# Pooled attention and maxout FFN: a hand-ordered program with groups of 64 tokens, the attention output of batches 2 to 7 transposed by the DMA crossbar

## The chip, the cores and the metric

One core of a Trainium2 chip. The time is the device time of one execution in microseconds (us); each kernel ran several times, in rounds beside the kernel before on the same chip. The kernel before took 288.1 to 290.7 us in all its executions. An execution over 1.5% above the fastest of its kernel is called slow; ratios use the others, the fast ones, alone. "The profile" is one execution taken by the hardware profiler; "the trace" is its list of instructions and transfers. Engines: PE = TensorE (PEld its weight loads), DVE = VectorE, ACT = ScalarE, POOL = GpSimd, SP = SyncE, which has no busy time on either page and issues transfers (161 before, 104 after the change). "SPq" or "ACTq" in a line is the transfer queue of that engine.

## The reference

K and V are averaged over 8 neighbouring tokens (576 become 72), each of 8 heads attends to the 72, and the result goes through three matrices whose products are maximised, and an output matrix.

```
q, k, v: (8 batches, 8 heads, 576, 64)          tokens: 8*576 = 4608, width 512
k_p, v_p = mean of 8 neighbours                 (8, 8, 72, 64)
attn = softmax(q @ k_p.T / 8)                   (8, 8, 576, 72)
x = (attn @ v_p), heads side by side            (4608, 512)
h = max(x @ w1, x @ w2, x @ w3)                 (4608, 768)
out = h @ w_out                                 (4608, 512)
```

## The kernel before

It works batch by batch: load, fold K and V over 8 neighbours (`fold`), transpose queries and keys, scores and exponentials (`heads`), products with V, normalisation and a TensorE transpose into `xT` (`values`). When 512 tokens are in `xT`, a group `moe(n)` follows: 72 matmuls with w1, w2, w3, then 24 with w_out. A scheduler orders each engine's instructions. These parts matter for the argument; cuts are marked.

```python
def load(b, after=None):
    kt = ld.tile([96, 6, POOL, D], F32, name="kt", tag="kt")      # ld: two buffers
    ...
    loads = [nc.sync.dma_start(out=kt, in_=ksrc)]                  # SyncE's queue
    loads.append(nc.sync.dma_start(out=vt, in_=vsrc))
    nc.gpsimd.dma_start(out=qb, in_=...)                           # converts to bf16
...
fold(nc.gpsimd, kt, [kp2[:, :, 0, :], kp2[:, :, 1, :]])            # b >= 2, on POOL
fold(nc.gpsimd, vt, [vp_all[:, b, :, 0:D]])
...
def values(b, ets):                                                # per chunk of 128 tokens
    ...                                                            # 8 matmuls, reciprocal
    xn = sb3.tile([128, 2, 4, D], F16, name="xn", tag="xn")        # sb3: three buffers
    nc.vector.tensor_tensor(out=xn, in0=..., in1=..., op=ALU.mult)
    for kc in range(KCH):
        nc.tensor.transpose(pxt[:, kc, :], xn[...], identh)        # four transposes
    nc.scalar.copy(out=xT[:, :, g0 + keep:g0 + 128], in_=pxt[:, :, keep:128])
...
def moe(n):
    ...                        # w1 part copied by ScalarE, two maxima by VectorE, then w_out
    for u in range(4):
        nc.sync.dma_start(out=dst[:, g, :], in_=osb[32 * u:32 * u + 32, :])
...
for b in range(B):
    loaded = first if b == 0 else load(b, w_dma[2])                # behind the weights
```

The softmax here doesn't subtract the row's maximum and nothing guards it: scores larger than these inputs give would overflow.

## Time and profile before

| | before |
|---|---|
| time, median | 289.3 us |
| profiled span | 288.2 us |
| first product with w1 starts | 43.97 us |
| last matmul ends | 281.3 us |
| TensorE's work between, at undisturbed distances | 226.4 of 237 us |
| SyncE's queue waiting for POOL's folds | 33 us |

The profile falls into a start that TensorE spends waiting for weights and keys, a body in which it is full, and an end of stores. The prediction shows the lines and reads them. "Undisturbed distance" is the time from the start of one matmul to the start of the next in a full stream (0.216 us at 512 columns, 0.056 us at 128). It is the measure used for TensorE throughout, as the durations that the profile gives overlap in a full stream: 379 ns for one of 512 columns, 219 ns for a transpose of 128 (medians).

### The profile page before, as it was taken

What the parts mean: (1) busy time and instruction counts of PE and PEld (TensorE: products, weight loads), DVE (VectorE), ACT (ScalarE), POOL (GpSimd) and SP (SyncE); (2) the same over time, 40 slices, a digit from 0 to 9 for tenths busy, and PEclk for the clock granted to TensorE, in tenths of its full rate; (3) what the DMA queues carried; (4) which work ended last, traced back from release to release, by engine and by line L of the source; (5) the groups of instructions that cost most, each with busy time, mean ns of one, the idle gap of its engine ahead of it and who ended that gap; (6) DMA issues with size and microseconds to landing.
All of it is one profiled execution on the core that took longest, in us unless ns stands there. A gap on an engine that the chain in (4) does not pass through costs nothing.

```text
span 288.2 us, 4331 instructions
## 1 busy us (share of the span) xinstructions
PE 248.6 (86%) x1664; PEld 131.2 (46%) x1664; DVE 129.3 (45%) x224; ACT 128.0 (44%) x218; POOL 117.4 (41%) x68
## 2 busy tenths in 40 slices
PE   0254049999999999999999999999999999999990
PEld 0132044564545455545554565456455544444440
DVE  7420083483238334724571557057505832533520
ACT  1134024753575267535753663565357533222230
POOL 6048006999999999999282300000000000000000
PEclk9999999999999999999999999999999999999996
DMA  7999999898839959975912700320040005014013
GB/s 189 255 228 199 261 239 229 190 219 234 193 111 216 202 141 214 235 174 119 206 31 72 141 20 0 98 50 0 2 123 23 2 9 138 1 27 120 3 45 102
DMA packets 17190, 36.47 MB, mean 127 GB/s; under 512 B 2736, under 2 KB 5040, under 8 KB 16496
## 3 DMA queue, kind: packets, MB, share of 16 engines
q1 hardware_dynamic: 12624, 28.32, 38.6%
q0 software_dynamic: 4544, 7.87, 15.3%
q8 instruction: 13, 0.21, 0.3%
q14 instruction: 9, 0.07, 0.1%
HBM read 34.60 MB, written 9.44 MB: 153 GB/s over the span
## 4 chain that ended last, share of the span: by engine, by line
PE 77%; DMA 14%; ACT 2%; DVE 1%; issue 1%; POOL 1%; SPq 0%; ACTq 0%; POOLq 0%
PE pw L194 47%; PE po L211 15%; DMA mw<-in_moe_w_dram 7%; PE psc L152 6%; PE pxt L179 4%; DMA out_dram<-osb 4%; DMA kt<-in_k_dram 3%; PE pav L166 3%; PE pqt L128 3%; ACT xT L183 2%; PE pkt L137 1%; DVE kt L108 1%; POOL mw L88 1%; ACT osb L215 0%; DVE xn L174 0%
## 5 line engine op out<-in xcount | busy, mean ns | idle before, releaser
L194 PE MATMUL pw<-xT,mw 128*128 128x512 f16 x648 | 163.8, 382 | 0.7 <-ACT xT L183 0.7
L194 PEld LDWEIGHTS <-mw 128*128 128x128 f16 x648 | 60.4, 98 | 51.0 <-issue 1.1
L202 DVE TENSOR_TENSOR t<-t,pw 128x512 f16<-128x512 f16 x54 | 37.1, 687 | 100.0 <-PE pw L194 97.6
L108 POOL TENSOR_TENSOR vt<-vt 72x2048 f32<-72x2048 f32 (+1 forms) x16 | 54.8, 3427 | 36.3 <-DMA vt<-in_v_dram 35.7
L199 ACT CAST t<-pw 128x512 f16<-128x512 f32 x54 | 31.6, 585 | 48.2 <-PE pw L194 47.7
L211 PE MATMUL po<-mwo,hT 128*128 128x512 f16 x216 | 48.1, 379 | 0.0
L205 DVE TENSOR_TENSOR hT<-t,pw 128x512 f16<-128x512 f16 x54 | 37.1, 686 | 16.5 <-PE pw L194 13.8
L155 ACT ACTIVATE et<-psc 72x576 f16<-72x576 f32 x64 | 37.4, 645 | 11.4 <-PE psc L152 11.3
L215 ACT COPY osb<-po 128x512 f32<-128x512 f32 x36 | 21.1, 587 | 36.2 <-PE po L211 34.7
L183 ACT COPY xT<-pxt 128x512 f16<-128x512 f16 (+1 forms) x40 | 21.8, 544 | 33.5 <-PE pxt L179 33.3
L211 PEld LDWEIGHTS <-hT 128*128 128x128 f16 x216 | 21.1, 98 | 25.5 <-DVE hT L205 1.7
L108 POOL TENSOR_TENSOR kt<-kt 96x1536 f32<-96x1536 f32 (+1 forms) x12 | 31.4, 2617 | 0.4
L152 PE MATMUL psc<-qT,kz 128*72 128x288 bf16 x128 | 27.9, 304 | 2.4 <-ACT et L155 1.5
L133 ACT COPY qT<-pqt 128x768 bf16<-128x768 bf16 x23 | 18.4, 801 | 24.0 <-PE pqt L128 23.7
L174 DVE TENSOR_TENSOR xn<-pav,rcp 128x512 f16<-128x512 f32 x40 | 26.7, 684 | 0.4
L179 PE MATMUL pxt<-identh,xn 128*128 128x128 f16 x160 | 16.5, 229 | 11.4 <-DVE xn L174 10.8
L128 PE MATMUL pqt<-ident,qb 128*128 128x128 bf16 x144 | 13.2, 234 | 13.7 <-DMA qb<-in_q_dram 12.0
L152 PEld LDWEIGHTS <-kz 128*72 128x72 bf16 x128 | 14.0, 117 | 19.5 <-issue 8.8
L179 PEld LDWEIGHTS <-xn 128*128 128x128 f16 x160 | 11.9, 102 | 21.9 <-DVE xn L174 17.4
L166 PE MATMUL pav<-vp,et 72*128 72x65 f16 x320 | 18.8, 200 | 3.3 <-POOL vp L111 3.3
L128 PEld LDWEIGHTS <-qb 128*128 128x128 bf16 x144 | 10.9, 105 | 20.5 <-DMA qb<-in_q_dram 12.0
L166 PEld LDWEIGHTS <-et 72*128 72x128 f16 x320 | 15.6, 103 | 7.3 <-ACT et L155 3.2
(23 smaller groups left out, 72.9 us busy)
## 6 DMA issues: line engine op xcount, KB each, us to landing
vt<-in_v_dram SPq DMA_DIRECT2D x8, 1152.0 KB
out_dram<-osb SPq DMA_DIRECT2D x144, 64.0 KB, 1.7
kt<-in_k_dram SPq DMA_DIRECT2D x7, 1152.0 KB, 10.4
qb<-in_q_dram POOLq DMA_DIRECT2D x8, 576.0 KB, 12.1
mw<-in_moe_w_dram POOLq DMA_DIRECT2D x3, 768.0 KB, 18.3
kt<-in_k_dram SPq DMA_DIRECT2D x2, 576.0 KB, 6.8
mwo<-in_moe_w_out_dram POOLq DMA_DIRECT2D x1, 768.0 KB, 25.4
```

Of the source, the lines that this page charges most:

```text
L108: e.tensor_tensor(out=t[:, :, 0:n, :], in0=t[:, :, 0:n, :], in1=t[:, :, n:2 * n, :], op=ALU.add)
L128: nc.tensor.transpose(pqt[:, u, :], qb[:, g, 2 * i:2 * i + 2, :], ident)
L152: nc.tensor.matmul(psc[:, par, 0:288], kz[:, par, h, :], mov, start=True, stop=True)
L155: nc.scalar.activation(out=et.rearrange("p (i a r) -> p i a r", a=2, r=NR), in_=psc[:, :, 0:288].rearrange("p a (i r) -> p i a r", r=NR), ...
L166: nc.tensor.matmul(pav[:, h // 4, 65 * (h % 4):65 * (h % 4) + 65], ets[h][:, c0:c0 + 128], vp_all[:, b, h, :], start=True, stop=True)
L179: nc.tensor.transpose(pxt[:, kc, :], xn[:, kc // 2, 2 * (kc % 2):2 * (kc % 2) + 2, :], identh)
L183: nc.scalar.copy(out=xT[:, :, g0 + keep:g0 + 128], in_=pxt[:, :, keep:128])
L194: nc.tensor.matmul(pw, w_sb[wi][:, kc, bass.ts(jc, 128)], xT[:, kc, col], start=(kc == 0), stop=(kc == KCH - 1))
L199: nc.scalar.copy(out=t, in_=pw)
L202: nc.vector.tensor_tensor(out=t1, in0=t, in1=pw, op=ALU.max)
L205: nc.vector.tensor_tensor(out=hT[:, jc, :], in0=t, in1=pw, op=ALU.max)
L211: nc.tensor.matmul(po, hT[:, jc, bass.ts(mm, 128)], wo_sb[:, jc, :], start=(jc == 0), stop=(jc == JCH - 1))
```

## The change

Its intent: start the first group earlier, by loading in smaller pieces in the order of need and by fixing every engine's order by hand; take stores in pieces of 64 rows; and take the transposes of the output off TensorE from batch 2 on. The crossbar transposes go out from SyncE, so the loads of K and V of batches 2 to 7 moved to ScalarE's queue. The diff, cut to what the argument touches:

```diff
-    NR = 32                                  # tokens of a query group
+    NR = 64
+    ctx.enter_context(tc.manual_schedule())  # program order is kept on each engine
...
+    for i in range(3):
+        load_w(slice(256 * i, 256 * i + 256))          # weights in thirds
...
-            kz[128, 2, H, 72]                          # keys as weights
+            kz[128, 2, H, 128]
...
+    def turn_x(b, c0, keep, xn, tag):
+        if b > 1:
+            g0 = S * b + c0
+            nc.sync.dma_start_transpose(
+                out=xT[:, :, g0 + keep:g0 + 128],
+                in_=xn.rearrange("p g h d -> p (g h d)")[keep:128])
+            return
+        ...                                            # batches 0 and 1: TensorE, as before
...
+    loads_on = nc.scalar
+    def load(b):
+        kts[b], x = load_kv(b, "kt", k, loads_on, F32, 1)
+        vts[b], y = load_kv(b, "vt", v, loads_on, F32, 1)
+        ...
+        load_q(b)
+    for slot, _ in enumerate(project(0, hT0)):         # output part of group 0
+        ...
+    load(2)
+    load(3)
+    fold_k(2, nc.gpsimd)
+    fold_v(2)
+    ...
+    for n in range(1, TOK // NB):                      # groups 1 to 8
+        if n + 2 < B:
+            fold_k(n + 2, nc.gpsimd)
+            fold_v(n + 2)
+        if n + 3 < B:
+            load(n + 3)
+        ...
+        for part in (hidden(n, hT), project(n, hT)):   # one "slot" per step of the group
+            for _ in part:
+                next(side, None)
+                ...                                    # a step of batch n + 1
+                slot += 1
```

## The prediction

> **What bounds the kernel now.** I read the page's busy line and its slices first, because they say which engine to count and when it starts.
>
> ```profile
> PE 248.6 (86%) x1664; PEld 131.2 (46%) x1664; DVE 129.3 (45%) x224; ACT 128.0 (44%) x218; POOL 117.4 (41%) x68
> ...
> PE   0254049999999999999999999999999999999990
> ```
>
> TensorE is full from the seventh slice to the last but one; before that, in some 44 us, it does little. Two phases, then: a start that is bound by something else, and a body bound by TensorE. The chain of waits, in order of time, names the something else and shows the pace of the body:
>
> ```profile
> 4.47 21.32 DMA mw<-in_moe_w_dram
> 25.81 9.92 DMA kt<-in_k_dram
> ...
> 43.97 0.59 PE pw L194
> ...
> 276.09 5.19 PE po L211 x24
> ```
>
> The start waits for weights and then for keys held back behind them; the first product with w1 starts at 43.97 us. The last line gives the true cost of a 512-column matmul in a full stream: 5.19/24 = 0.216 us, not the 0.38 us that the group list shows as one's duration (that one includes the pipeline). Distances between starts in the same trace give 0.056 us for a 128-column transpose, 0.122 us for a 288-column score, 0.033 us for a value product of 65 columns. From 43.97 us to the last matmul's end at 281.3 us these distances account for 226.4 of 237 us; the other 11 us are small gaps, the largest sort (36 times about 0.08 us) ahead of scores with 72-column weights. The end, from the timeline:
>
> ```profile
> 278.03 7.56 SPq L219 DMA_DIRECT2D out_dram<-osb  x16
> 281.35 0.59 ACT L215 COPY osb<-po 128x512 f32<-128x512 f32 x1 [0.75 <-PE po L211]
> ```
>
> Sixteen stores of 64 KB go out one after the other at 0.47 us, so the span ends 6.9 us after the last matmul. The reported time is 1.1 us over the profiled span (289.3 against 288.2).
>
> Two more views matter for what the change moves: POOL's folds of V by shape, and what the DMA queue on SyncE waited for.
>
> ```profile
> L108 POOL TENSOR_TENSOR vt<-vt 72x2048 f32<-72x2048 f32 x8 | 36.1, 4508 | 35.7 <-DMA vt<-in_v_dram 35.7
> L108 POOL TENSOR_TENSOR vt<-vt 72x1024 f32<-72x1024 f32 x8 | 18.8, 2347 | 0.6
> L111 POOL TENSOR_TENSOR vp<-vt 72x512 f16<-72x512 f32 x8 | 10.1, 1267 | 0.6
> ...
> SPq L66 <- POOL kp L111: 16.7, 2, 9.1
> SPq L67 <- POOL vp L111: 16.6, 3, 8.3
> ```
>
> A fold of V costs 8.1 us of POOL. The loads of K and V into a double buffer wait for such folds (33 us in five waits). This costs nothing today: only stores stand behind them, on a queue that computes nothing.
>
> [...] 72-column weights load in 117 ns, 128-column ones in 98 ns.
>
> **The change part by part.**
>
> 1. *Start.* K, Q and V of batch 0 are loaded first, then the weights in column thirds, and the first two groups' first products run on half groups. Loading cost from the packets: converting packets take 98, 134 and 191 ns for 1024, 1536 and 2304 bytes written, a line of 23 + 0.073 ns per byte, so about 61 ns for the new 512-byte packets and 107 for 1152. Over 16 engines, q, k and v of batch 0 cost 3.4 + 3.2 + 3.5 us, one third of the weights 5.8 us. With packets of the converting queue starting near 6 us, batch 0 is in by some 13 us and the first third by some 20. Behind that: exponentials of batch 0 until about 18, then two output chunks (reciprocal 0.2, multiply 0.68, transpose, copy 0.59). **First product at about 22.5 us**, 21.5 earlier.
> 2. *Group 0.* 72 products x 0.216 = 15.6, three remaining chunks of batch 0 1.5, pooling K of batch 1 on TensorE (8 x 0.216) 1.7, its query transposes 1.0, waits 1.7: to 44. By the same packet sum w_out lands near 42 to 44. Output part: 24 x 0.216 = 5.2, scores 2.0, pooling V (16 half-width) 1.7, waits 1.5: to 54.4; its last copy ends at about **55**.
> 3. *The new wait.* In the built order of the changed kernel the loads of batches 2 and 3 stand on **ScalarE's** queue behind that copy (SyncE is kept for the transposes), and the loads of batch 4 at the head of group 1, waiting for POOL, ahead of the first evacuation of group 1. Batch 4 reuses the buffers of batch 2, so ScalarE stands still until batch 2 is loaded (6.5 us: 0.4 issue, 4.6 for 576 packets of 2 KB at about 128 ns on 16 engines, the rest latency), K folded (now 72 x 2048: 4.5 + 2.35 + 2 x 1.27 = 9.4) and V folded (8.1): 24 us. Then a copy, a maximum and two key copies (0.4 + 0.4 + 1.5) before TensorE goes on: **27 us**, of which TensorE uses 3.3. Later loads wait for folds that ended long before.
> 4. *TensorE's remaining work* after 55 us: 8 groups x 96 x 0.216 = 165.9; six batches at 18 x 0.056 + 8 x 0.033 + 8 x 0.25 + 40 x 0.033 = 4.6, in all 27.5; batch 1's outputs 2.4: 195.8, less the 3.3. The crossbar removes 120 transposes x 0.056 = **6.7 us** from TensorE and 30 copies of 0.37 to 0.59 us from ScalarE, which wasn't the bound.
> 5. *Gaps.* The 78 ns ones go with 128-column keys. But in a fixed order the first query transposes come one slot (0.86 us) after the key transposes whose two copies take 1.5 us; with the following query copies about 1.5 us per batch. I take 10 us in all, as now.
> 6. *End.* Two stores instead of four behind the last copy: 5 us instead of 6.9.
>
> Sum: 55 + 27 + 192.5 + 10 + 5 = 289.5; 1 for late transposes; 1.1 for the reported time: **291.5 us**. So the start gains 21.5, the end 2, the transposes 6.7, and almost all of it goes into one wait.
>
> **The rivals.** (a) *The wait is short or absent*, because loads land or folds run sooner than I think. POOL's fold times are steady in the trace (4.49 and 4.51 us), and the built order is plain, which speaks against it; without the wait, the sum would be about 267. Half of it would give 279. (b) *The crossbar is slow.* A chunk's normalised output has three buffers, so the fourth waits on VectorE for the first's transpose; between them are five slots, about 4.2 us of slack. With a latency of 7 us VectorE, and soon TensorE, would lose some 2 us in each of six batches: about 303. Nothing in the trace before speaks for or against it. (c) *The start is no faster*, as the small weight packets are slower than the line says, or w_out comes late: each us there adds one, likely 3 to 5, so 295.
>
> **Range and chances.** Without (b) the error is that of the start (3 us), of the wait (3) and of the gaps (4), about 6 us together; (b) stretches the upper side. Range 283 to 303. Two per cent below is 283.5 and above is 295.1: faster 0.15, same 0.5, slower 0.35.
>
> **What would show it.** Right: first w1 product at 20 to 25 us; one hole of more than 20 us on TensorE soon after the first output part, and in the waits a ScalarE queue entry for POOL's fold of V; POOL busy without pause through it; no further hole over 2 us; crossbar transposes landing within about 4 us. Wrong: no such hole (then well under 283), or TensorE pausing in each group for a transpose (then over 300), or a first product after 30 us.

The five terms make 289.5, and with 1 and 1.1 that is 291.6, put as 291.5. In step 3 "the rest latency", some 1.5 us, is the author's estimate; in the trace before, a store of 64 KB took 1.7 us from issue to landing. That the gaps of 78 ns go with 128-column keys (step 5) is the author's estimate too, from the two load times.

## The result, and the profile after

The changed kernel took **304.5 us** (median; 303.6 to 306.6) against 289.3 us: ratio 1.053, 95% interval 1.047 to 1.059. A ratio here is the mean time of one kernel's fast runs over that of the other's of the same rounds, so it is not quite the ratio of the medians. The profiled execution was the slowest of the four, 306.6 us with a span of 304.8 us.

The busy line, TensorE's slices and the granted clock of the changed kernel (slices of 7.6 us):

```profile
PE 257.1 (84%) x1733; PEld 138.6 (45%) x1733; DVE 126.0 (41%) x230; ACT 118.0 (39%) x194; POOL 123.2 (40%) x73
...
PE   6598989430079995799999699999999999999993
PEclk9759999955558999799999779999999999999999
```

TensorE now works from the first slice on, but there is a hole (a stretch in which TensorE does nothing) in slices 8 to 11, and smaller dips in slices 16 and 23. Below the hole the granted clock drops to 5 tenths, and it stays there when work is back in slice 12. What ScalarE did through the hole, its timeline between 55 and 90 us (start, duration, what; in brackets the idle time before and what ended it):

```profile
56.09 0.61 ACTq L70 DMA_DIRECT2D kt<-in_k_dram  x1
...
58.56 5.83 ACTq L70 DMA_DIRECT2D vt<-in_v_dram  x1
64.43 0.59 ACT L210 COPY xT<-pxt 128x512 f16<-128x512 f16 x1 [7.86 <-DMA out_dram<-osb]
65.69 0.59 ACT L210 COPY xT<-pxt 128x512 f16<-128x512 f16 x1 [0.67 <-PE pxt L206]
75.33 0.31 ACTq L70 DMA_DIRECT2D kt<-in_k_dram  x1
83.53 0.31 ACTq L70 DMA_DIRECT2D vt<-in_v_dram  x1
83.94 0.37 ACT L271 CAST t<-pw 128x256 f16<-128x256 f32 x1 [17.66 <-POOL vp L121]
```

Four loads go out from 56.09 us; the fourth keeps the queue for 5.83 us. Then two copies, and the load of K of batch 4 leaves at 75.33 us and that of V at 83.53 us. Only then does ScalarE evacuate the first product of group 1. The chain of waits gives the folds that the two loads stood for:

```profile
65.83 4.50 POOL kt L118
70.41 2.35 POOL kt L118
72.82 2.48 POOL kp L121 x2
75.30 4.46 POOL vt L118
79.83 2.33 POOL vt L118
82.24 1.27 POOL vp L121
84.85 0.64 PE pkt L157 x8
```

K of batch 2 is folded at 75.30 us, V at 83.51 us, and TensorE's key transposes start at 84.85 us. This is the wait of the prediction. The two smaller dips, in TensorE's timeline, and ScalarE's copy ahead of the first of them:

```profile
124.11 0.59 PE L150 MATMUL pqt<-ident,qb 128*128 128x128 bf16 x6 [4.00 <-ACT qT L152]
...
172.97 3.17 PE L296 MATMUL po<-mwo,hT 128*128 128x512 f16 x7 [2.74 <-DVE hT L277]
```

```profile
122.37 0.31 ACTq L70 DMA_DIRECT2D vt<-in_v_dram  x1
122.77 0.59 ACT L271 CAST t<-pw 128x512 f16<-128x512 f32 x1 [6.53 <-DMA out_dram<-osb]
```

In the first, ScalarE stood 6.5 us at the load of V of batch 5, not for a fold but for a *store*: by the trace's records, the transfers from SyncE and ScalarE take eight semaphores in turn (108, 111 and 113 to 118), this load's semaphore (117) was last given to a store that SyncE had sent at 115.70 us, and the load left at 122.37 us, after that store had landed at 122.27 us. In the second, VectorE's list of waits has this:

```profile
DVE xn L223 <- DMA xT<-xn: 3.4, 1, 3.4
```

It stood 3.4 us for a buffer that a crossbar transpose was still reading. The chain of waits shows that store and this transpose, each with its start and its time to landing:

```profile
115.70 6.57 DMA out_dram<-osb
152.46 18.28 DMA xT<-xn
```

The crossbar's time to landing, asked for two stretches of the changed kernel: 100 to 127 us, where loads are in flight for the most part, and 195 to 265 us, where the last of them lands at 200.5 us.

```profile
xT<-xn SPq DMA_TRANSPOSE x5, 7.5
```

```profile
xT<-xn SPq DMA_TRANSPOSE x15, 2.4
```

The view knows the landing of only one transpose in each stretch, so each of these medians is a single transfer. The updates of the semaphores in the same trace, 16 after each transpose, give all thirty: 17 met no load and landed in 2.3 to 4.1 us (median 2.45); 13 met a load of K, V or Q and took 2.5 to 18.3 us (median 5.8). It isn't the crossbar alone: counted in the same way, stores of 128 KB landed in 2.2 to 3.4 us without a load in flight, and in up to 15.2 us when sent beside the loads of K, V and Q of batches 2 to 7. And the granted clock after the long hole, in two windows (us of the stretch, then busy time and count per engine, clock, share of the transfer engines, GB/s):

```profile
85.00:93.00 8.00, 7.26 (x57) 5.66 (x56) 2.83 (x7) 2.93 (x5) 7.84 (x5) 0.50 0.79 184
93.00:115.00 22.00, 21.91 (x164) 12.50 (x161) 11.29 (x23) 10.26 (x18) 21.66 (x9) 0.99 0.42 81
```

For 8 us after the hole TensorE runs at a clock of 0.50; by the trace's records it does so from the hole's end at 84.85 to 93.64 us, 8.8 us, and is busy for 8.05 of them. Four matmuls of 256 columns, one slot's worth, take 0.85 us in the chain of waits at 85.49 us and 0.43 us at the full clock.

### The profile page after: what moved, and what is told of

It is laid out like the page before. It is cut to its first block, busy times and chain, and to the rows that moved or that the text cites. A ratio compares the mean times of both kernels' runs of the same rounds, so it can differ in the third digit from the quotient of the medians.

```text
span 304.8 us, 4463 instructions
## 1 busy us (share of the span) xinstructions
PE 257.1 (84%) x1733; PEld 138.6 (45%) x1733; DVE 126.0 (41%) x230; ACT 118.0 (39%) x194; POOL 123.2 (40%) x73
## 3 DMA queue, kind: packets, MB, share of 16 engines
q0 software_dynamic: 12144, 9.64, 21.9%
## 4 chain that ended last, share of the span: by engine, by line
PE 70%; DMA 10%; POOL 6%; DVE 6%; issue 4%; ACT 2%; SPq 1%; ACTq 0%; DVEq 0%; POOLq 0%
PE pw L266 39%; PE po L296 14%; DMA xT<-xn 6%; PE psc L180 5%; PE pqt L150 3%; PE pav L215 3%; POOL kt L118 2%; POOL vt L118 2%; DMA out_dram<-osb 2%; DMA kt<-in_k_dram 2%; PE pvp L139 2%; DVE kz L160 1%; DVE kt L118 1%; DVE xn L223 1%; PE pkt L157 1%
## 5 line engine op out<-in xcount | busy, mean ns | idle before, releaser
L266 PE MATMUL pw<-xT,mw 128*128 128x512 f16 (+1 forms) x696 | 163.3, 372 | 3.0 <-ACT xT L210 1.3
L274 DVE TENSOR_TENSOR t<-t,pw 128x512 f16<-128x512 f16 (+1 forms) x58 | 37.7, 651 | 86.8 <-PE pw L266 43.6
L271 ACT CAST t<-pw 128x512 f16<-128x512 f32 (+1 forms) x58 | 32.3, 557 | 77.7 <-PE pw L266 49.9
L118 POOL TENSOR_TENSOR kt<-kt 72x2048 f32<-72x2048 f32 (+1 forms) x12 | 41.1, 3428 | 27.5 <-issue 21.3
L185 ACT ACTIVATE et<-psc 72x576 f16<-72x576 f32 (+2 forms) x62 | 40.7, 663 | 18.8 <-PE psc L180 18.7
L277 DVE TENSOR_TENSOR hT<-t,pw 128x512 f16<-128x512 f16 (+1 forms) x58 | 37.7, 649 | 13.2 <-PE pw L266 10.4
L118 POOL TENSOR_TENSOR vt<-vt 72x2048 f32<-72x2048 f32 (+1 forms) x12 | 41.1, 3425 | 1.3 <-DMA vt<-in_v_dram 0.9
L180 PE MATMUL psc<-qT,kz 128*128 128x64 bf16 (+3 forms) x192 | 27.4, 258 | 1.9 <-DVE qT L152 1.3
L180 PEld LDWEIGHTS <-kz 128*128 128x128 bf16 x192 | 19.2, 102 | 17.3 <-issue 2.8
L152 ACT COPY qT<-pqt 128x768 bf16<-128x768 bf16 (+2 forms) x23 | 18.1, 786 | 14.3 <-PE pqt L150 14.2
L215 PE MATMUL pav<-vp,et 72*128 72x65 f16 x320 | 17.7, 199 | 0.1
```

The lines of the kernel that those rows point to most:

```text
L118: e.tensor_tensor(out=t[:, :, 0:n, :], in0=t[:, :, 0:n, :], in1=t[:, :, n:2 * n, :], op=ALU.add)
L180: nc.tensor.matmul(out, kz_all[b % 2][:, f % 2, h, :], qTs[b][:, n + i0:n + i1, 64 * (h % 2):64 * (h % 2) + 64], start=True, stop=True)
L185: nc.scalar.activation(out=out, in_=in_, func=FT.Exp, scale=1.0 / 64.0)
L215: nc.tensor.matmul(pav[:, h // 4, 65 * (h % 4):65 * (h % 4) + 65], ets[b][:, h, c0:c0 + 128], vp_all[:, b, h, :], start=True, stop=True)
L266: nc.tensor.matmul(pw, w_sb[wi][:, kc, bass.ts(jc, 128)], xT[:, kc, col], start=(kc == 0), stop=(kc == KCH - 1))
L271: nc.scalar.copy(out=t, in_=pw)
```

## The experiments

Theory A: a transfer issued from ScalarE that must wait (for a fold of POOL, or for a store's semaphore) holds ScalarE, and with it TensorE. Theory B: the crossbar transposes and the loads slow each other, whichever queue issues them. All results were correct. "Before" took 289.0 to 289.9 us (medians) in the experiments. The table has medians of all four runs; e10_v_later and e4_four_xn have one slow run each and e8_pool_loads two, which the ratios leave out.

| run | change to the changed kernel | us | ratio to before, 95% interval |
|---|---|---|---|
| changed kernel | | 304.5 | 1.053 (1.047 to 1.059) |
| e2_sync_loads | loads from SyncE | 290.6 | 1.002 (0.997 to 1.008) |
| e10_v_later | V of batch 4 later | 293.4 | 1.012 (1.008 to 1.016) |
| e12_v5_later | V of batch 5 later | 300.8 | 1.038 (1.031 to 1.045) |
| e3_mid_loads | loads of batches 4 to 7 later | 297.3 | 1.026 (1.020 to 1.031) |
| e4_four_xn | four `xn` buffers | 297.1 | 1.024 (1.018 to 1.030) |
| e1_tensor_turns | no crossbar | 298.7 | 1.031 (1.029 to 1.034) |
| e5_early_sync | loads from SyncE, batch 2 early | 278.7 | 0.963 (0.959 to 0.966) |
| e6_early_tensor | e5, no crossbar | 279.1 | 0.963 (0.960 to 0.966) |
| e7_from_batch3 | e5, crossbar from batch 3 | **274.1** | **0.946** (0.945 to 0.948) |
| e8_pool_loads | e5, loads from POOL | 289.8 | 0.994 (0.986 to 1.002) |
| e11_pool_from3 | e8, crossbar from batch 3 | 281.6 | 0.973 (0.966 to 0.979) |
| e9_before_crossbar | *kernel before*, crossbar from batch 2 | 293.9 | 1.014 (1.009 to 1.019) |

### Who issues the loads

```diff
-    loads_on = nc.scalar
+    loads_on = nc.sync
```

> The changed kernel with the loads of batches 2 to 7 issued from SyncE's queue in place of ScalarE's, at the same places of the program. Theory A (ScalarE stands still because a DMA issue in its queue waits, first for POOL's fold of V of batch 2, then at the head of group 2 for a store to land): the hole before the key transposes of batch 2 ends when POOL's fold of K is done, near 75 us instead of 85, and the 4 us hole near 120 us goes: 288 to 292 us. Theory B (the loads land late and the crossbar transposes and stores are slowed by them, whichever queue issues): as the changed kernel, 302 to 307 us.

290.6 us, as theory A has it. TensorE's timeline at the end of its hole, in this run:

```profile
74.53 0.66 PE L157 MATMUL pkt<-ident,kp 72*128 72x72 bf16 x8 [16.15 <-POOL kp L121]
```

The hole now ends with the fold of K, 10.3 us sooner than in the profile of the changed kernel (2.5 us of that is an earlier first product). There is no pause of 7 us in front of it, and none of 4 us near 120 us; a hole of 3.0 us at 105 us, at a crossbar transpose, is new. The 5.83 us that ScalarE lost to its fourth load thus lay in the shadow of the same fold and, as far as this comparison shows, cost nothing by themselves; why that issue took so long stays open.

### One load at a time

```diff
-        if n + 3 < B:
+        if n + 3 < B and n > 1:
             load(n + 3)
+        if n == 1:
+            kts[4], _ = load_kv(4, "kt", k, loads_on, F32, 1)
...
                 slot += 1
+                if n == 1 and slot == 16:
+                    vts[4], _ = load_kv(4, "vt", v, loads_on, F32, 1)
+                    load_q(4)
```

> The changed kernel with one load moved: that of V of batch 4, sixteen slots into group 1 instead of its head (the load of K of batch 4 stays at the head, and all other loads where they were). Theory A: ScalarE then waits for the fold of K of batch 2 alone (near 75 us) and not for that of V (near 83.5), and TensorE goes on 8 us sooner: 294 to 299 us. Rival: the hole lasts as long as the loads need to land, and it stays at 302 to 306 us.

293.4 us (292.1 to 294.2 in the three fast runs), a little faster than expected. This is the narrowest test of the main step: one load moved on ScalarE's queue (that of Q moves in the text, but keeps its place in POOL's order), and the wait for the fold of V is gone.

```profile
75.20 0.64 PE L157 MATMUL pkt<-ident,kp 72*128 72x72 bf16 x8 [7.94 <-ACT xT L210]
```

Key transposes at 75.20 us against 84.85 us (1.2 us of it from the start). The load of V of batch 5, in the same way:

```diff
-        if n + 3 < B:
+        if n + 3 < B and n != 2:
             load(n + 3)
+        if n == 2:
+            kts[5], _ = load_kv(5, "kt", k, loads_on, F32, 1)
...
                 slot += 1
+                if n == 2 and slot == 6:
+                    vts[5], _ = load_kv(5, "vt", v, loads_on, F32, 1)
+                    load_q(5)
```

> The changed kernel with one load moved: that of V of batch 5, six slots into group 2 instead of its head, where its issue on ScalarE waited 6.6 us for the semaphore of a store that SyncE had just sent. If that wait makes the hole of 4.2 us near 120 us (and the slow clock after it): 297 to 301 us, no hole over 1.5 us there. Rival (TensorE waits there for something that lands late whoever waits, the stores or the crossbar): 303 to 306 us.

300.8 us; no hole over 1 us is left between 87 and 161 us. So the wait for the store's semaphore is a cause too, of some 4 us (all four runs lie under all four of the changed kernel). The load had nothing to do with that store but the semaphore.

```diff
-        if n + 3 < B:
-            load(n + 3)
...
                 slot += 1
+                if n + 3 < B and slot == (16 if n == 1 else 6):
+                    load(n + 3)
```

> The changed kernel with the loads of batches 4 to 7 still on ScalarE's queue but issued six slots into a group (sixteen into the first) and not at its head. Theory A: POOL's fold of V is over when ScalarE reaches the issue and the stores of the group before have landed, so ScalarE does not stand still: the long hole ends near 75 us and the one near 120 us goes, 288 to 293 us. Theory B: no change, or worse as the loads now run beside the transposes at the group's end: 303 to 310 us.

297.3 us, a miss: 4 us slower than theory A allowed. The long hole ended at 74.7 us as expected, but a new one of 8.9 us came at the end of group 1, where the loads now ran beside the crossbar. VectorE's waits for it, in this run (total, times, longest):

```profile
DVE xn L223 <- DMA xT<-xn: 23.8, 4, 8.7
```

Theory A is right about the wait that it names, and theory B in one direction: loads slow the transposes. That transposes slow the loads is not shown; the V loads of batches 5 to 7 landed 17.3 to 17.6 us after their issue without the crossbar (e1_tensor_turns) and 16.9 to 17.5 us with it (e5_early_sync).

### The crossbar

```diff
-    xn = sb3.tile([128, 2, 4, D], F16, name="xn", tag="xn")
+    xn = sb3.tile([128, 2, 4, D], F16, name="xn", tag="xn", bufs=4)
```

> The changed kernel with four buffers for the normalised output in place of three, so that VectorE may run one chunk further ahead of the crossbar. If the hole of 2.9 us in group 3 is VectorE's wait for a crossbar transpose: it shrinks or goes, 300 to 304 us, with VectorE's wait for the crossbar near zero. Rival: the same 2.9 us appears as TensorE's wait for the transposed columns, no change.

297.1 us (294.6 to 297.5, and a slow run of 301.8), under its range: faster by more than the hole of 2.9 us and the slow clock after it explain. The hole in group 3 is gone from its trace, one of 1.9 us has come near 173 us, and VectorE's waits for the crossbar are down to 0.6 us in all. Between the two profiled executions, most of the rest has nothing to do with the buffer: the first product comes 1.7 us sooner, and the clock is back 3.5 us after the long hole, not 8.8. That second time has two lengths in the traces: 8.5 to 9.3 us in the changed kernel and in the runs e1 to e3, 3.1 to 4.4 us in e4_four_xn, e10_v_later and e12_v5_later. At half the clock that is some 2.5 us of difference, whatever the edit. What decides between them is not shown.

```diff
-        if b > 1:
+        if b > B:            # never: all output transposes on TensorE
```

> The changed kernel with its loads left on ScalarE's queue and all output transposes back on TensorE. Theory A (ScalarE's queue makes the loss, the crossbar only some of it): the long hole before 85 us stays, TensorE gets 6.7 us of work back and loses the 3 us hole and the slow clock after it in group 3, and the stores at the head of group 2 may land sooner: 299 to 307 us. Theory B (the crossbar transposes make the loss): under 293 us.

298.7 us, just under the range of theory A. With 6.7 us more work on TensorE it is 5.8 us faster: in this program the crossbar cost about 12 us. Its trace has no hole over 1 us after 87 us. The load of V of batch 5 didn't wait there either: without the thirty crossbar transposes the eight semaphores fall to other transfers, and this load, issued at 115.17 us, got one whose store had landed at 114.08 us. So some 4 of the 12 us are that accident of the semaphores, not the crossbar's own time.

```diff
+            if b > 1:                                    # in the kernel before
+                g0 = S * b + c0
+                nc.sync.dma_start_transpose(out=xT[:, :, g0 + keep:g0 + 128],
+                    in_=xn.rearrange("p g h d -> p (g h d)")[keep:128])
+                continue
```

> The kernel before with one part of the change alone: the output of batches 2 to 7 transposed by the crossbar, from SyncE's queue, where its loads wait for folds. If only TensorE's instructions count: 289.3 - 6.7, 281 to 284 us. If the transposes stand behind waiting loads and their packets on that queue (theory B's form here): 288 to 310 us.

293.9 us: this part of the change alone slows the kernel before by 1.4% (its interval is clear of 1), though it takes 6.7 us from TensorE. Its trace has new holes of 1.6 to 3.3 us in four places, and VectorE waits 10.7 us for the crossbar, in seven waits.

### Loads in time

```diff
+    loads_on = nc.sync
+    def load(b): ...                 # as before, moved up
+    load(2)
+    fold_k(2, nc.gpsimd)
+    fold_v(2)
     out0 = outputs(0, (PW, PW, TR, TR, TR))
...
-    load(2)
     load(3)
-    fold_k(2, nc.gpsimd)
-    fold_v(2)
```

> Loads from SyncE's queue, and those of batch 2 and its folds put ahead of the output chunks of batch 0, so that they run during group 0. Theory A: the key fold of batch 2 is done before TensorE asks for it (near 57 us), so the holes at 58 to 65 and 69 to 85 us go, with the slow clock after them: 264 to 272 us. Theory B (crossbar and loads in each other's way): the holes of the later groups stay or grow, 280 us or more.

278.7 us, faster than the kernel before but 7 us slower than theory A's range and under theory B's. K of batch 2 is folded by 58.9 us and the long hole is gone. In its place one of 9.1 us in the output part of group 1; SyncE's queue and VectorE's timeline in that run:

```profile
68.07 0.45 SPq L70 DMA_DIRECT2D vt<-in_v_dram  x1
77.72 7.84 SPq L200 DMA_TRANSPOSE xT<-xn  x2
```

```profile
91.89 0.69 DVE L223 TENSOR_TENSOR xn<-pav,rcp 128x512 f16<-128x512 f32 x1 [8.91 <-DMA xT<-xn]
```

Two transposes sent from 77.72 us on, ten us behind three loads of 1152 KB (the last is shown), free VectorE's buffer only by 91.9 us. By their semaphores the last load landed at 91.28 us and the two transposes at 91.80 and 93.49 us. With all transposes on TensorE instead:

> As e5_early_sync, with all transposes of the output back on TensorE. If the crossbar is worth what it takes from TensorE (120 transposes of 56 ns) and costs no waits, this is 5 to 8 us slower than e5_early_sync: 270 to 279 us. If the crossbar costs waits (theory B), this is faster than e5_early_sync.

279.1 us: neither faster nor slower than e5_early_sync. The crossbar gives 6.7 us and takes back about as much. So, the crossbar without batch 2, whose transposes met those three loads:

```diff
-        if b > 1:
+        if b > 2:
```

> e5_early_sync with the crossbar for batches 3 to 7 alone; batch 2, whose transposes stood behind 2.3 MB of loads on SyncE's queue and cost a hole of 9 us, goes back to TensorE. If that hole was the crossbar's price: 278.7 - 9.1 + 20 transposes of 56 ns and up to 3 us for stores behind the same loads, 270 to 275 us, faster than both e5_early_sync and e6_early_tensor. If the crossbar waits elsewhere too: 277 us or more.

**274.1 us**, 5.4% faster than the kernel before and 10% faster than the changed kernel (274.06/304.54): the best of all, with runs of 273.7 to 274.1 us. Loads are not out of the crossbar's way here: by the semaphores four transposes of batches 4 and 5 took 6.2 to 8.2 us beside loads, and VectorE waited 6.5 us for the crossbar, in two waits. But no gap of TensorE at a crossbar transpose is over 0.5 us; the slack covers them. Its TensorE slices (6.8 us each):

```profile
PE   7598989968999799999999999999999999999993
```

Is it the order in SyncE's queue that hurts the transposes, or the load in flight as such? Loads from POOL's queue tell:

```diff
-    loads_on = nc.sync
+    loads_on = nc.gpsimd
```

> e5_early_sync with the loads of batches 2 to 7 issued from POOL's queue, so that neither stores nor crossbar transposes stand behind them in SyncE's queue. If the 9 us hole of group 1 comes from that order in the queue: it goes, 267 to 274 us. If it comes from sharing the transfer engines with a load in flight: it stays at 5 us or more, 274 to 281 us.

289.8 us (286.1 and 289.1 in the two fast runs, up to 296.5 in the slow ones), outside both ranges. On POOL's queue each load stands behind a fold, so it comes later (in the twin run below those of K of batches 3 to 7 left 9 to 30 us later than in e5_early_sync) and runs beside the transposes. The profiled execution was slow, so its holes are not used; the twin run with TensorE for batch 2 was fast:

> As e8_pool_loads, with batch 2 transposed on TensorE and the crossbar for batches 3 to 7. If the order in the queue was the cause in e5_early_sync, the same as e8_pool_loads within 2 us. If a load in flight is the cause, faster than e8_pool_loads by 3 us or more, 268 to 274 us.

281.6 us: 6 us faster than e8_pool_loads (fast runs with fast runs), as a load in flight would have it, but over that range of 268 to 274 us, and 7.5 us slower than e7_from_batch3, with the same crossbar transposes. Its VectorE waits for them:

```profile
DVE xn L223 <- DMA xT<-xn: 23.8, 4, 8.6
```

No store and no transpose stands behind a load in SyncE's queue here, and the waits are there. A load in flight is enough. TensorE has holes of 2.7 and 3.7 us from it. The two runs don't exclude that the order in the queue adds to it.

## Why the prediction was wrong

The sum of the prediction beside the profile of the changed kernel (us; from its slowest run):

| term | predicted | measured |
|---|---|---|
| first product with w1 | 22.5 | 25.0 |
| last copy of group 0 ends | 55 | 56.6 |
| wait, to the first query transposes of batch 2 | 27, to 82 | 30, to 86.6 |
| TensorE's work from there | 192.5 | 191.4 |
| gaps in it | 10, and 1 for late transposes | 21.9 |
| end | 5 | 4.9 |
| reported time over span | 1.1 | 1.8 |
| sum | 291.5 | 306.6 |

1. *Start*: right in mechanism, 2.5 us late in this run; in the other runs with the same start the first product came at 22.5 to 24.2 us.
2. *Group 0*: right, within 2 us.
3. *The new wait*: right, as the built order told it; e10_v_later shows it. The folds took 9.5 and 8.2 us, against 9.4 and 8.1. Too small was the load of batch 2: from 56.1 us to the fold's start at 65.8 us, 9.7 us instead of 6.5. The load takes that long by itself: in e7_from_batch3 one of K took 9.3 us (56.19 to 65.47 us) with no other load in flight, and the 16 transfer engines were busy for 0.65 of that time. The prediction had spread its packets over all 16 without a pause.
4. **The step that failed** is its last sentence, "Later loads wait for folds that ended long before". They did not wait for folds, but the load of V of batch 5 waited for the semaphore of a store: a hole of 4.2 us in TensorE at the head of group 2. I had looked for the waits on buffers and passed over the other semaphores in the same list. e12_v5_later shows what it was worth. By size the step "gaps" failed too: it takes the most of the 15 us between the two sums (next point).
5. *Gaps*: 10 us were predicted and 21.9 measured. Of these, waits of over 0.3 us are 12.4: the 4.2 us just named, 2.9 us in group 3 by the crossbar, 1.2 us for a store that had not yet freed its buffer, and 0.3 to 0.9 us a time for the copies of keys, queries and outputs. Matmuls at twice their undisturbed distance make 8.6 us: after each of the three holes over 2 us that this trace has from 69 us on (the long one, 4.2 and 2.9 us) the clock was 0.50, until 93.6, 127.8 and 179.0 us. My sum had no term for the clock. A full group of the later part had gaps of only some 1 us, less than the 1.5 I took.
6. *The crossbar* (rival b): I expected its cost in each batch or nowhere. It came where loads were in flight, with up to 18.3 us to landing, and not after 200.5 us, where no load was left and all transposes landed in 2.3 to 4.1 us. The latency of "within about 4 us", named as a sign of being right, thus held without loads and failed beside them. The "1 for late transposes" was too small, and the 6.7 us on the gain side bought nothing in this program: e1_tensor_turns is faster without the crossbar, e9_before_crossbar slower with it.
7. *The end*: right, 4.9 us.

Rival (a), no wait, would have made "about 267"; e5_early_sync without the wait took 278.7 and e7_from_batch3 274.1 us. For e5_early_sync the gap is the hole of 9.1 us at the crossbar, with 3.6 us of slow clock. For e7_from_batch3 it is the clock: 6.7 us of slow matmuls, most of them at a clock of 0.50 from 58.6 to 68.8 us, where no gap of TensorE is over 0.8 us. So a long hole is not all that brings the slow clock; what does is not shown.

## What to carry to other kernels

A transfer issued from a computing engine's queue brought all its waits to that engine: on ScalarE 17.7 us of idle time that a fold ended, for its buffer, and 6.5 us for its semaphore. The choice of the queue made 14 us (304.5 to 290.6 us in e2_sync_loads). The transfer itself was much the same from each queue: the V loads of batches 5 to 7 landed 16.0 to 17.6 us after their issue from ScalarE in e1_tensor_turns, from SyncE in e5_early_sync and from POOL in e11_pool_from3. List both waits for each such issue in the built order, or issue it from a queue on which nothing urgent stands. And a resource that looks free (the crossbar) was not free beside the transfers that feed the kernel (2.3 to 4.1 us to landing without a load in flight, 2.5 to 18.3 us beside one): it is worth what it saves only where the time to landing beside a load fits before its result or its buffer is needed. Of the four programs with it that have a twin without it, it paid in one: e7_from_batch3, from batch 3 on, 5.0 us against e6_early_tensor.
